# Local and pooled attention with a dense layer behind it: q and k of two more groups transposed by DMA, less slack behind transfers that VectorE reads, and new tables of who copies what

## The chip, the core and the metric

The kernel runs on one core of a Trainium2 chip. The metric is the device time of one execution in microseconds (us). The profile shows one such execution by engine: PE is TensorE, PEld its weight loads, DVE is VectorE, ACT is ScalarE, POOL is GpSimd and SP is SyncE, which here issues every transfer.

## The reference

q, k and v have the shape (8, 8, 576, 64): 8 batches, 8 heads, 576 positions, 64 wide. Each head's attention is the sum of two parts, and a dense layer follows.

```python
# pooled: mean over 4 neighbours, full attention over 144 positions, repeated 4 times
q_d = q.reshape(B, H, Sd, 4, D).mean(axis=3)          # k_d and v_d likewise
out_up = np.repeat(sm_attn(q_d, k_d, v_d), 4, axis=2)
# local: only positions with |i - j| < 4
scores = np.where(mask, scale * q @ k.T, -1e9)
out_local = softmax(scores) @ v
x = (out_up + out_local)      # as (4608 tokens, 512)
# dense
h = x @ w_in                  # 512 -> 2048
g = h - np.tanh(h)
return g @ w_out              # 2048 -> 512
```

## The kernel before

The 64 heads are worked on in 32 pairs (p), two pairs making a group (n), 16 groups in all. The instructions are not written in their final order. Each goes into a list with its engine, an assumed duration and what it reads and writes, and a list scheduler then lays down one fixed order for each engine. The scheduler's view of a transfer is its cost, a fixed 1800 ns, and a slack that keeps the reader from being placed too near:

```python
LAT = {"PE": 270, "ACT": 150, "DVE": 110, "POOL": 150, "SP": 50, "DMA": 1800}
...
lag = self.LAT[eng]
if self.ops[u][4] < 5000:                     # the reader's priority
    lag += self.spare(self.ops[u][4], eng, self.ops[u][0])
...
def spare(pri, eng, to):
    if eng == "DMA":
        return 2500 if pri >= 140 else 1500 if pri >= 80 else 0
    level = (pri >= 120) + (pri >= LATER)     # LATER = 180
    return SPARE[to == "PE"].get(eng, (0, 0, 0))[level]
```

An attention pair has priority 10 p, the turn of a group's q and k 20 n, their loads' readers 20 n - 12. The dense matmuls have priority 5000, so they fill what attention leaves.

**q and k.** They are loaded with rows of nine positions (qkn), cast and reordered to bf16 (`reorder`, line 494, into qr) and then transposed (`turn`). Up to group FI - 1 TensorE does it, nine transposes into a PSUM bank; from group FI on it is a DMA transpose into a v buffer (vst) that is not needed any more. A copy with a strided read brings either into qk, and two sums make the pooled q and k:

```python
def turn(n, i):                               # i = 0: q and k of one half, 1: the other
    ps, po, ts, ox = banks_of(2 * n + i)
    if (n, i) in TB:
        ps, ts = po, ox                       # through ps_ox in place of ps_ts
    if n >= FI:
        b16 = vst[4 + i] ...
        op("SP", 900, lambda: nc.sync.dma_start_transpose(out=b16..., in_=qr[s][:, i]...), ...)
        op("DMA", T_IN, None, ..., pri=pri)
    def tr():
        for a in range(A6):                   # nine; line 523
            T.transpose(b16[:, 128*a:128*a+128], qr[s][:, i, a, :], ident)
    ...                                       # copy, line 532: whole or in two halves (TS)
    ...                                       # add1 line 536, add2 line 541: sums of 4 (AS, AD)
```

For groups from FI on, v has four buffers in place of six (`slot_v`).

**One pair.** Scores of the local part (`s1`, line 590) go into ps_ts, those of the last tile and the pooled part (`s2`, lines 590 and 609) into the same bank or, from pair MERGE on, into ps_ox, in one block with the next pair's `s1`. ScalarE takes the exponential (lines 626, 652, 655), VectorE multiplies by the mask (630, 659). The output matmuls (`outs`, lines 672 and 678) write ps_ox; VectorE takes the reciprocal (689) and normalises into ln (691). The way back to xT is one of three:

```python
if p >= XOUT:                                 # XOUT = 12
    nc.sync.dma_start_transpose(out=lnT[sl], in_=ln[sl]...)     # then two adds, line 711
elif p in UP:                                 # matmuls that add both parts (726, 731), copy (737)
else:                                         # transposes (747 to 751), copy (754), add (756)
```

**Dense.** For each block of 512 tokens, `mm1` makes 16 times four 128x512 matmuls (line 781), followed by tanh (789) and the subtraction into gT (792), and `mm2` makes the second product (line 835), copied out by ScalarE (846). Four PSUM banks, `ps_hy`, serve both. While attention's first pairs run, ps_ts1 and ps_ox1 stand there; the dense part takes these over in two halves, a tile for each bank (`dense_banks`). Line 1069 is a filler matmul on a constant, placed where the scheduler sees TensorE idle ahead of the dense part.

Of the kernel before, what the change touches and what calls it, by code (L numbers as in the profile page):

```python
# [11 lines left out]
ALU = mybir.AluOpType  # L12
# [3 lines left out]
class Program:  # L16
# [20 lines left out]
    def op(self, eng, ns, fn, reads=(), writes=(), pri=0):  # L37
        i = len(self.ops)
        deps = set()
        for key in reads:  # L40
            if key in self.last_write:
                deps.add(self.last_write[key])
        for key in writes:
            if key in self.last_write:
                deps.add(self.last_write[key])
            deps.update(self.readers.get(key, ()))
        for key in reads:
            self.readers.setdefault(key, set()).add(i)
        for key in writes:
            self.last_write[key] = i  # L50
            self.readers[key] = set()
        deps.discard(i)
        self.ops.append((eng, ns, fn, deps, pri))
        self.touch.append(set(reads) | set(writes))
        return i
# [108 lines left out]
def kernel(  # L164
# [55 lines left out]
    vd = fixed("vd", [128, 2, 4, 65], BF16, NVW)  # L220
# [7 lines left out]
    lnT = fixed("lnT", [128, 7, 128], BF16, NLN)  # L228
    od = fixed("od", [128, G], BF16, 2)
# [25 lines left out]
    P = Program()  # L255

    def spare(pri, eng, to):
        if eng == "DMA":
            return 2500 if pri >= 140 else 1500 if pri >= 80 else 0
        level = (pri >= 120) + (pri >= LATER)  # L260
        return SPARE[to == "PE"].get(eng, (0, 0, 0))[level]
    LATER = 180
    SPARE = ({"POOL": (0, 500, 1000)},
             {"POOL": (0, 1000, 1500), "DVE": (0, 300, 800), "ACT": (0, 200, 500)})
    P.spare = spare
    op = P.op
    V, A, T, GP = nc.vector, nc.scalar, nc.tensor, nc.gpsimd
# [174 lines left out]
    def prep_v(p):  # L442
# [4 lines left out]
            out=vw[w][:, 2 * jj:2 * jj + 2, :, 0:64], in_=vst[s]))  # L447
                  for eng, ns, fn in CAST_V[CV.get(p, 1)]],
                 reads=[("vst", s, 0), ("vst", s, 1)],
# [49 lines left out]
    def turn(n, i):  # L499
# [4 lines left out]
        ps, po, ts, ox = banks_of(2 * n + i)  # L504
        if (n, i) in TB:
            ps, ts = po, ox
# [60 lines left out]
    def attention(p):  # L567
        b, j, hb, s, jj = p // NP, p % NP, p // 2, p % 2, p % 2
        w, sq, y, sl = hb % NVW, (p // 2) % 2, p % 2, p % NLN
        ps, po, ts, ox = banks_of(p)  # L570
        pri = 10 * p
# [47 lines left out]
        if p <= MERGE:  # L619
# [3 lines left out]
        e1 = E[se][:, 0:960].rearrange("p (h c) -> p h c", h=2)  # L623
# [4 lines left out]
           reads=ts, writes=[("E", se, 0)], pri=URG.get("e1", {}).get(p, pri))  # L628
        if not first:
# [3 lines left out]
                op=ALU.mult), reads=["mask"], writes=[("E", se, 0)], pri=pri)  # L633
# [11 lines left out]
        else:  # L645
            op("PE", 380 * cold, s2, reads=qks + qkds, writes=ox if p >= MERGE else ts,
               pri=pri)
        P.has(p // 2, ("qk", sq, 0), ("qk", sq, 1))
        if MERGE <= p < NPAIR - 1:
# [4 lines left out]
           reads=sb, writes=[("E", se, 1)], pri=URG.get("e2", {}).get(p, pri))  # L654
        op("ACT", 655, lambda: A.activation(
            out=e3, in_=pb[:, :, 96:384], func=AF.Exp, scale=SCALE / 16.0),
           reads=sb, writes=[("E", se, 2)], pri=URG.get("e2", {}).get(p, pri))
        if not first:
# [3 lines left out]
                op=ALU.mult), reads=["mask"], writes=[("E", se, 1)], pri=pri)  # L662
# [5 lines left out]
        def outs():  # L668
# [17 lines left out]
           reads=[("E", se, 0), ("E", se, 1), ("E", se, 2), ("vw", w, jj), ("vd", w)],  # L686
           writes=ox, pri=late)
        blocks = po[:, :, 0:455].rearrange("p h (n c) -> p h n c", c=65)
        op("DVE", 240, lambda: V.reciprocal(out=r[s], in_=blocks[:, :, :, 64]),
           reads=ox, writes=[("r", s)], pri=late)  # L690
# [4 lines left out]
            op=ALU.mult), reads=ox + [("r", s)], writes=[("ln", sl)],  # L695
           pri=URG.get("norm", {}).get(p, late))


        xo = xT[j][:, b * S:(b + 1) * S]
        if p >= XOUT:  # L700
            op("SP", 450, lambda: nc.sync.dma_start_transpose(
                out=lnT[sl], in_=ln[sl].rearrange("p n c -> p (n c)")),
               reads=[("ln", sl)], writes=[("lnT", sl), ("q", ("lnT", sl)), ("fl", p)],
               pri=pri - 60)
            op("DMA", T_OUT, None, reads=[("q", ("lnT", sl)), ("ln", sl)],
               writes=[("lnT", sl)], pri=pri)
            for t0, nt, n, up in ((0, 4, 120, lnT[sl][:, 5, 0:120]),
                                  (4, 1, 96, lnT[sl][:, 6, 104:128])):
                g = n // 4
                P.choice([(name, ns[t0 > 0], lambda eng=eng, t0=t0, nt=nt, n=n, g=g,  # L710
                           up=up: eng.tensor_tensor(  # L711
                    out=xo[:, QW * t0:QW * t0 + nt * n].rearrange(
                        "p (t g a) -> p t g a", t=nt, a=4),
                    in0=lnT[sl][:, t0:t0 + nt, 0:n].rearrange(
                        "p t (g a) -> p t g a", a=4),
                    in1=up[:, 0:nt * g].rearrange("p (t g) -> p t g", g=g).unsqueeze(3)
                    .to_broadcast([128, nt, g, 4]), op=ALU.add))
                          for name, ns, eng in XADD],
                         reads=[("lnT", sl)], writes=[("x", b, j)], pri=pri)
            return  # L720


        if p in UP:
# [11 lines left out]
            for m, (i0, i1) in enumerate([(0, 1), (1, 2)] if parted else [(0, 2)]):  # L735
# [4 lines left out]
                         reads=ox, writes=[(("x", "xh")[m], b, j)],  # L740
                         pri=URG.get("add", {}).get(p, late))
# [4 lines left out]
        def back():  # L746
# [8 lines left out]
           reads=ox, writes=[("od", s)], pri=URG.get("od", {}).get(p, late))  # L755
# [4 lines left out]
           reads=ox + [("od", s)], writes=[("x", b, j)],  # L760
           pri=URG.get("add", {}).get(p, late))
# [92 lines left out]
    def dense(kb):  # L854
# [18 lines left out]
        if kb == NBLK:  # L873
# [2 lines left out]

    M2_FIRST = 16
    XOUT, T_OUT, AHEAD = 12, 1600, 7
    P_A, LATE = 5000, {0: 40, 2: 40, 3: 40}
    MERGE, GV = 14, 7  # L880
    FI, T_IN = 11, 2050
    XADD = [("DVE", (800, 350), V)]
    ORDER, W_FIRST = '0g123', '0123qv'
    TB = {(1, 0), (1, 1), (2, 0), (2, 1), (3, 0), (5, 0)}
    PV = {2: 0, 3: 1, 4: -1, 5: 0, 6: 1}
    PLACE = {2: (0, 2), 3: (1, 2), 4: (4, 4), 5: (1, 2), 6: (4, 4), 7: (1, 1), 8: (3, 3)}
    W_LATE = [0, 0, 0, 0]
    T_QK, T_V, T_W, W_PRI = 900, 780, 2750, 53
    CAST = [("POOL", 620, GP.tensor_copy), ("ACT", 620, A.copy),
# [1 line left out]
    CAST_V = [[("POOL", 790, GP.tensor_copy), ("ACT", 720, A.copy)],  # L891
              [("POOL", 790, GP.tensor_copy)], [("ACT", 720, A.copy)],
              [("DVE", 500, V.tensor_copy)]]
    CV = {0: 3, 1: 1, 2: 1, 3: 3, 4: 1, 5: 0, 6: 3, 7: 0, 8: 2, 9: 0, 10: 2, 11: 3}
    REORDER = [[("DVE", 860, V.tensor_copy), ("ACT", 950, A.copy),
                ("POOL", 1350, GP.tensor_copy)],
               [("DVE", 860, V.tensor_copy)], [("ACT", 950, A.copy)],
               [("DVE", 1150, V.tensor_copy)], [("POOL", 1350, GP.tensor_copy)]]
    RE = {(0, 0): 1, (0, 1): 4, (1, 0): 2, (1, 1): 4, (2, 0): 3, (2, 1): 4, (3, 0): 0, (3,
          1): 0, (4, 0): 2, (4, 1): 4, (5, 0): 1, (5, 1): 1}  # L900
    TURN = [[("ACT", 1125, A.copy), ("DVE", 1250, V.tensor_copy)],
            [("ACT", 1125, A.copy)], [("DVE", 1250, V.tensor_copy)],
            [("ACT", 2210, A.copy)]]
    TU = {(0, 0): 2, (0, 1): 1, (1, 0): 2, (1, 1): 1, (2, 0): 1, (2, 1): 1, (3, 0): 2, (3,
          1): 1, (4, 0): 1, (4, 1): 1, (5, 0): 1, (5, 1): 1}
    re_v, re_a, re_p = (("DVE", 480, V.tensor_copy), ("ACT", 580, A.copy),
                        ("POOL", 720, GP.tensor_copy))
    REORDER_H = [[[re_v, re_a, re_p]] * 2, [[re_v], [re_a]], [[re_v], [re_p]],
# [1 line left out]
    POOLED = [[("ACT", 600, A.copy), ("DVE", 650, V.tensor_copy)],  # L910
              [("ACT", 600, A.copy)], [("DVE", 650, V.tensor_copy)]]
    PV1 = False
    VD = {0: 2, 1: 0, 2: 1, 3: 1, 4: 1, 5: 0, 6: 1}
    RS = {(0, 1): 2, (1, 0): 4, (1, 1): 3, (3, 0): 4}
    UP = {0: 3, 1: 0, 2: 3, 3: 3, 4: 2, 6: 3, 8: 1, 11: 3}
    UP_COPY = [("ACT", 660, A.copy), ("DVE", 720, V.tensor_copy)]
    UP_H = [[("ACT", 370, A.copy)], [("DVE", 410, V.tensor_copy)]]
    half_v, half_p = ("DVE", 420, 260, V), ("POOL", 650, 500, GP)
# [2 lines left out]
              [[("DVE", 700, V.tensor_copy)], [("ACT", 640, A.copy)]]]  # L921
    ADD_H = [[[half_v, half_p]] * 2, [[half_v], [half_p]], [[half_v], [half_v]],
             [[half_p], [half_p]]]
    TS = {(0, 0): 1, (0, 1): 2, (1, 1): 2, (2, 1): 2, (5, 0): 1, (5, 1): 3}
    AS = {(0, 0): 1, (1, 0): 1, (1, 1): 1, (2, 0): 1, (4, 0): 1, (5, 0): 4, (5, 1): 4, (6,
          1): 1}
    URG = {'e1': {8: -2, 9: -2, 10: -2, 11: -2}, 'e2': {0: -2, 1: -2, 2: -2, 3: -2, 4: -2,
          5: -2, 6: -2, 7: -2, 8: -2, 9: -2, 10: -2, 11: -2}, 'od': {0: -2, 1: -2}, 'norm':
          {0: -2, 1: -2, 2: -2, 3: -2, 4: -2, 5: -2, 6: -2, 7: -2, 8: -2, 9: -2, 10: -2, 11:
          -2}, 'add': {0: -2, 1: -2, 2: -2, 3: -2, 4: -2, 5: -2, 6: -2, 7: -2}, 'turn': {4:  # L930
          -2, 5: -2}, 'vd': {2: -2, 3: -2}}
    ADDERS = [[("DVE", 760, 440, V), ("POOL", 1190, 850, GP)],
              [("POOL", 1190, 880, GP)], [("DVE", 760, 440, V)]]
    AD = {(0, 0): 2, (0, 1): 2, (1, 0): 0, (1, 1): 1, (2, 0): 0, (2, 1): 1, (3, 0): 0, (3,
          1): 1, (4, 0): 0, (4, 1): 0, (5, 0): 2, (5, 1): 1}

    op("DVE", 180, lambda: V.memset(warm, 0.0), writes=["warm"], pri=-999)
    op("POOL", 500, c_ident, writes=["ident"], pri=-99)
# [5 lines left out]
    for i in range(2):  # L944
        def guards(i=i):
# [3 lines left out]
           writes=[("qk", i, a, y) for a in range(2) for y in range(2)])  # L949
    for i in range(NVW):  # L950
        def ones(i=i):
# [3 lines left out]
           writes=[("vd", i), ("vw", i, 0), ("vw", i, 1)])  # L955
# [3 lines left out]
           writes=[("vd", i)], pri=-96)  # L959
# [69 lines left out]
    for p in range(NPAIR):  # L1029
        n = p // 2  # L1030
        if p % 2 == 0 and 1 < n < GV and PV.get(n, 0) == 0:
            pool_v(n)
# [4 lines left out]
        def turns(at):  # L1037
            for m in range(max(n + 1, 2), min(n + 3, NGRP)):
                for i in range(2):
                    if 4 * m - 5 + PLACE.get(m, (0, 1))[i] == at:  # L1040
                        reorder(m, i)
                        turn(m, i)
        turns(2 * p)
        if p % 2 == 0 and 1 < n < GV and PV.get(n, 0) == 1:
            pool_v(n)
# [9 lines left out]
        if p % NP == NP - 1:  # L1055
            b = p // NP
# [44 lines left out]
```

## Time and profile before

| What | Value |
|---|---|
| time, median of 3 (lowest, highest) | 338.79 us (337.65, 339.12) |
| span of the profiled execution | 335.9 us |
| VectorE, subtraction into gT (L792) | 144, 684 ns each |
| ScalarE, tanh (L789) | 144, 601 ns each |
| q/k transposes on TensorE (L523) | 198 |
| q/k transposes by DMA (L514) | 10, landing 4.3 us after issue |
| transposes back by DMA (L701) | 20, landing 3.0 us after issue |
| transfers on SyncE's queue | 60.04 MB, 66.7% of 16 engines |

A row of the table of groups reads: line, engine, operation, what it writes and reads, how many | busy us, mean ns of one | idle time of the engine just before it, and what ended it. In a timeline a row is start, length, engine, line and operation; a bracket at its end is how long the engine stood idle before it, and behind what. Consecutive matmuls overlap in the records, so the pace of TensorE is read from starts.

### The profile page before, as it was taken

The numbers are of one execution on the slowest core, as the hardware profiler recorded it, in microseconds if no ns is written. First come the engines' busy times: TensorE is split into PE (matmuls) and PEld (weight loads), VectorE is DVE, ScalarE is ACT, GpSimd is POOL, SyncE is SP. The second block draws the span as 40 slices with busy tenths as digits, with TensorE's granted clock in tenths as the row PEclk, the third lists the DMA queues.
The fourth block names the chain that finished last, engine by engine and source line by source line (L and its number), as shares of the span: only waits on it lengthen the run. The fifth ranks groups of instructions, "written<-read, shape, count | busy, mean of one in ns | idle before, by whom it ended". The sixth has DMA issues, their size and how long they took to land.

```text
span 335.9 us, 6861 instructions
## 1 busy us (share of the span) xinstructions
PE 322.9 (96%) x2602; PEld 167.8 (50%) x2602; DVE 236.0 (70%) x388; ACT 211.2 (63%) x341; POOL 153.0 (46%) x181
## 2 busy tenths in 40 slices
PE   8778999989998999999999999999999999999996
PEld 5454554655554455554444544444444444444444
DVE  3788897679998888989797878787666444343300
ACT  1765878777848578667869695987554334344421
POOL 8564565349499488794948476653000000000000
PEclk9999999999999999999999999999999999999999
DMA  6999999999952799899899979843223100100012
GB/s 208 263 379 311 318 320 303 241 283 295 291 177 75 187 210 282 202 218 280 212 246 276 195 228 225 173 94 92 59 61 86 34 31 31 62 33 31 31 66 93
DMA packets 96878, 60.47 MB, mean 180 GB/s; under 512 B 74510, under 2 KB 80078, under 8 KB 96846
## 3 DMA queue, kind: packets, MB, share of 16 engines
q1 hardware_dynamic: 96846, 60.04, 66.7%
q8 instruction: 20, 0.33, 0.5%
q14 instruction: 12, 0.10, 0.1%
HBM read 43.05 MB, written 9.44 MB: 156 GB/s over the span
## 4 chain that ended last, share of the span: by engine, by line
PE 84%; DVE 10%; POOL 2%; issue 2%; ACT 1%; POOLq 0%; DVEq 0%
PE ps_hy L835 34%; PE ps_hy L781 33%; DVE ln L691 3%; PE ps_ox L672 3%; PE ps_ts L590 3%; PE ps_ts L523 2%; PE ps_ox L678 2%; PE ps_ts L1069 2%; DVE gT L792 2%; DVE qk L532 2%; PE ps_hy L810 1%; PE ps_ox L465 1%; DVE E L630 1%; POOL half L536 1%; ACT qk L532 1%
## 5 line engine op out<-in xcount | busy, mean ns | idle before, releaser
L781 PE MATMUL ps_hy<-xT,w_in_sb 128*128 128x512 bf16 x576 | 145.2, 379 | 0.6 <-DVE gT L792 0.4
L835 PE MATMUL ps_hy<-w_out_sb,gT 128*128 128x512 bf16 x560 | 140.4, 379 | 0.0
L792 DVE TENSOR_TENSOR gT<-ps_hy,uy 128x512 bf16<-128x512 f32 x144 | 94.9, 684 | 56.8 <-ACT uy L789 56.6
L789 ACT ACTIVATE uy<-ps_hy 128x512 f32<-128x512 f32 x144 | 83.0, 601 | 60.6 <-PE ps_hy L781 58.3
L781 PEld LDWEIGHTS <-w_in_sb 128*128 128x128 bf16 x576 | 53.1, 98 | 60.4 <-issue 1.8
L835 PEld LDWEIGHTS <-gT 128*128 128x128 bf16 x560 | 52.3, 98 | 57.6
L536 POOL TENSOR_TENSOR half<-qk 128x576 f32<-128x576 bf16 (+1 forms) x32 | 32.6, 1021 | 49.3 <-ACT qk L532 38.9
L691 DVE TENSOR_TENSOR ln<-ps_ox,r 128x896 bf16<-128x896 f32 x30 | 32.7, 1089 | 0.8
L626 ACT ACTIVATE E<-ps_ts 128x960 bf16<-128x960 f32 x30 | 29.4, 981 | 2.5 <-PE ps_ts L590 2.5
L846 ACT COPY uy<-ps_hy 128x512 f32<-128x512 f32 x35 | 20.6, 590 | 14.3 <-PE ps_hy L835 14.2
L630 DVE TENSOR_TENSOR E<-E,mask 128x960 bf16<-128x960 bf16 x28 | 24.5, 874 | 5.5 <-ACT E L626 5.4
L532 ACT COPY qk<-ps_ts 128x1152 bf16<-128x1152 bf16 (+1 forms) x16 | 16.5, 1034 | 18.0 <-PE ps_ts L523 8.3
L711 DVE TENSOR_TENSOR xT<-lnT 128x480 bf16<-128x480 bf16 (+1 forms) x40 | 27.6, 705 | 0.0
L359 POOL TENSOR_TENSOR qkn<-qkn 128x512 f32<-128x512 f32 (+1 forms) x18 | 25.8, 1432 | 3.3 <-DMA qkn<-in_v_dram 2.6
L446 POOL CAST vw<-vst 128x640 bf16<-128x640 f32 x26 | 22.9, 885 | 6.9 <-DMA vst<-in_v_dram 3.6
L494 POOL CAST qr<-qkn 128x1152 bf16<-128x1152 f32 (+1 forms) x16 | 19.4, 1214 | 8.4 <-DMA qkn<-in_k_dram 5.6
L532 ACT COPY qk<-vst 128x1152 bf16<-128x1152 bf16 x10 | 22.1, 2209 | 0.9 <-POOL half L536 0.9
L541 POOL TENSOR_TENSOR qkd<-half 128x288 bf16<-128x288 f32 (+1 forms) x32 | 21.4, 673 | 1.6 <-DVE half L536 0.4
L672 PE MATMUL ps_ox<-vw,E 128*128 128x65 bf16 x300 | 18.2, 194 | 1.9 <-DVE qk L532 1.0
L672 PEld LDWEIGHTS <-E 128*128 128x128 bf16 x300 | 15.4, 98 | 9.0 <-issue 2.3
L590 PEld LDWEIGHTS <-qk 64*128 64x128 bf16 x320 | 9.6, 95 | 18.2 <-issue 15.2
L494 DVE CAST qr<-qkn 128x1152 bf16<-128x1152 f32 (+1 forms) x16 | 15.4, 965 | 2.2 <-DMA qkn<-in_q_dram 2.2
(106 smaller groups left out, 294.5 us busy)
## 6 DMA issues: line engine op xcount, KB each, us to landing
vst<-in_v_dram SPq DMA_DIRECT2D x62, 160.0 KB, 4.9
qkn<-in_q_dram SPq DMA_DIRECT2D x32, 288.0 KB, 4.1
qkn<-in_k_dram SPq DMA_DIRECT2D x32, 288.0 KB, 4.9
out_dram<-uy SPq DMA_DIRECT2D x35, 256.0 KB, 3.5
qkn<-in_v_dram SPq DMA_DIRECT2D x9, 512.0 KB, 5.1
gT<-in_moe_w_in_dram SPq DMA_DIRECT2D x4, 1024.0 KB, 9.1
xT<-in_moe_w_out_dram SPq DMA_DIRECT2D x8, 256.0 KB, 4.6
gT<-in_moe_w_out_dram SPq DMA_DIRECT2D x2, 1024.0 KB, 8.9
```

The costliest lines, as they stand in the source:

```text
L494: P.choice([(eng, ns, lambda fn=fn, x0=x0, x1=x1: fn(out=dst[:, x0:x1], in_=srt[:, x0:x1])) for eng, ns, fn in table], reads=[("qkn", sn, ...
L532: fn(out=o[:, ys].rearrange("p y (g a) -> p y g a", a=A6), in_=b16.rearrange("p (a g y) -> p y g a", a=A6, y=2)[:, ys])
L536: eng.tensor_tensor(out=half[:, ys], in0=four[:, ys, :, 0:2], in1=four[:, ys, :, 2:4], op=ALU.add)
L626: op("ACT", 980, lambda: A.activation(out=e1, in_=ps[:, :, 0:480], func=AF.Exp, scale=SCALE), reads=ts, writes=[("E", se, 0)], pri=URG.get ...
L630: op("DVE", 900, lambda: V.tensor_tensor(out=e1, in0=e1, in1=mask[:, 0:480].unsqueeze(1).to_broadcast([128, 2, 480]), op=ALU.mult), reads= ...
L672: T.matmul(po[:, hh, 65 * t:65 * t + 65], E[se][:, c:c + 128], vw[w][:, 2 * jj + hh, t, :], start=True, stop=True)
L691: op("DVE", 1090, lambda: V.tensor_tensor(out=ln[sl].rearrange("p n (h d) -> p h n d", d=D), in0=blocks[:, :, :, 0:64], in1=r[s].unsqueeze ...
L711: up=up: eng.tensor_tensor(out=xo[:, QW * t0:QW * t0 + nt * n].rearrange("p (t g a) -> p t g a", t=nt, a=4), in0=lnT[sl][:, t0:t0 + nt, 0: ...
L781: T.matmul(ps_hy[slot], w_in_sb[:, dc, fc * 128:(fc + 1) * 128], xT[dc][:, kb * 512:kb * 512 + 512], start=(dc == 0), stop=(dc == N_DC - 1))
L789: op("ACT", 490, lambda: A.activation(out=u[us], in_=ps_hy[slot], func=AF.Tanh), reads=[("hy", slot)], writes=[("u", us)], pri=-1)
L792: op("DVE", 620, lambda: V.tensor_tensor(out=gT[g][:, fc, :], in0=ps_hy[slot], in1=u[us], op=ALU.subtract), reads=[("hy", slot), ("u", us) ...
L835: T.matmul(ps_hy[slot], gT[g][:, fc, ts * 128:ts * 128 + 128], w_out_sb[:, fc, :], start=(fc == 0), stop=(fc == N_FF - 1))
```

## The change

Two more groups, 9 and 10, have q and k transposed by DMA (FI from 11 to 9). A transfer that VectorE reads gets a slack of 1000 ns where it had 1500 or 2500; readers on other engines keep theirs. Scores are merged from pair 13 in place of 14 (MERGE). The turn of group 5 leaves ps_ox (TB). The pairs whose outputs are held back at the start are 1 and 2 with priority 25, where they were 0, 2 and 3 with 40 (LATE). The remaining tables say which engine copies or adds which group's data, whole or in halves, where in the program a turn is written down, and what is urgent; they are drawn anew so that the order fits the new slack. The purpose is to take transposes off TensorE and to let the DMA transposes back be used sooner.

```diff
     def spare(pri, eng, to):
+        if eng == "DMA" and to == "DVE":
+            return NEAR if pri >= 80 else 0
         if eng == "DMA":
             return 2500 if pri >= 140 else 1500 if pri >= 80 else 0
...
-    LATER = 180
+    LATER = 200
+    NEAR = 1000
...
-    P_A, LATE = 5000, {0: 40, 2: 40, 3: 40}
-    MERGE, GV = 14, 7
-    FI, T_IN = 11, 2050
-    XADD = [("DVE", (800, 350), V)]
+    P_A, LATE = 5000, {1: 25, 2: 25}
+    MERGE, GV = 13, 7
+    FI, T_IN = 9, 2050
...
-    TB = {(1, 0), (1, 1), (2, 0), (2, 1), (3, 0), (5, 0)}
-    PV = {2: 0, 3: 1, 4: -1, 5: 0, 6: 1}
-    PLACE = {2: (0, 2), 3: (1, 2), 4: (4, 4), 5: (1, 2), 6: (4, 4), 7: (1, 1), 8: (3, 3)}
+    TB = {(1, 0), (1, 1), (2, 0), (2, 1), (3, 0)}
+    PV = {2: 0, 3: 0, 4: -1, 5: -1, 6: 0}
+    PLACE = {2: (0, 0), 3: (1, 2), 4: (4, 4), 5: (1, 2), 6: (4, 4), 7: (1, 1), 8: (2, 2)}
...                      # CV, RE, TU, VD: who casts v, reorders, copies a turn, pooled v
-    UP = {0: 3, 1: 0, 2: 3, 3: 3, 4: 2, 6: 3, 8: 1, 11: 3}
+    UP = {0: 2, 1: 0, 2: 1, 3: 3, 4: 2, 6: 3, 8: 0, 11: 3}
...
-    TS = {(0, 0): 1, (0, 1): 2, (1, 1): 2, (2, 1): 2, (5, 0): 1, (5, 1): 3}
+    TS = {(0, 0): 3, (0, 1): 1, (1, 1): 1, (2, 1): 1, (4, 0): 1, (4, 1): 3, (5, 0): 3, (5,
+          1): 2, (6, 1): 1}
...                      # RS, AS, AD: halves of the reorder, who adds; URG: what is urgent
```

The choice in XADD had one entry, VectorE, and becomes a plain instruction on VectorE. In UP, 3 is a copy in two halves on ScalarE and VectorE, 1 a whole copy on ScalarE, 2 a whole one on VectorE, 0 leaves it to the scheduler.

More of the change, by code (lines that the diff above doesn't have):

```diff
@@ L709, in attention @@
                 g = n // 4
-                P.choice([(name, ns[t0 > 0], lambda eng=eng, t0=t0, nt=nt, n=n, g=g,
-                           up=up: eng.tensor_tensor(
+                op("DVE", (800, 350)[t0 > 0], lambda t0=t0, nt=nt, n=n, g=g, up=up: V.tensor_tensor(
                     out=xo[:, QW * t0:QW * t0 + nt * n].rearrange(
@@ L716, in attention @@
                     in1=up[:, 0:nt * g].rearrange("p (t g) -> p t g", g=g).unsqueeze(3)
-                    .to_broadcast([128, nt, g, 4]), op=ALU.add))
-                          for name, ns, eng in XADD],
-                         reads=[("lnT", sl)], writes=[("x", b, j)], pri=pri)
+                    .to_broadcast([128, nt, g, 4]), op=ALU.add),
+                   reads=[("lnT", sl)], writes=[("x", b, j)], pri=pri)
             return
@@ L893 @@
               [("DVE", 500, V.tensor_copy)]]
-    CV = {0: 3, 1: 1, 2: 1, 3: 3, 4: 1, 5: 0, 6: 3, 7: 0, 8: 2, 9: 0, 10: 2, 11: 3}
+    CV = {0: 3, 1: 1, 2: 2, 3: 3, 4: 0, 5: 1, 6: 3, 7: 1, 8: 2, 9: 0, 10: 0, 11: 3}
     REORDER = [[("DVE", 860, V.tensor_copy), ("ACT", 950, A.copy),
@@ L898 @@
                [("DVE", 1150, V.tensor_copy)], [("POOL", 1350, GP.tensor_copy)]]
-    RE = {(0, 0): 1, (0, 1): 4, (1, 0): 2, (1, 1): 4, (2, 0): 3, (2, 1): 4, (3, 0): 0, (3,
-          1): 0, (4, 0): 2, (4, 1): 4, (5, 0): 1, (5, 1): 1}
+    RE = {(0, 0): 0, (0, 1): 1, (1, 0): 4, (1, 1): 2, (2, 0): 1, (2, 1): 0, (3, 0): 4, (3,
+          1): 0, (4, 0): 2, (4, 1): 4, (5, 0): 0, (5, 1): 1}
     TURN = [[("ACT", 1125, A.copy), ("DVE", 1250, V.tensor_copy)],
@@ L903 @@
             [("ACT", 2210, A.copy)]]
-    TU = {(0, 0): 2, (0, 1): 1, (1, 0): 2, (1, 1): 1, (2, 0): 1, (2, 1): 1, (3, 0): 2, (3,
-          1): 1, (4, 0): 1, (4, 1): 1, (5, 0): 1, (5, 1): 1}
+    TU = {(0, 0): 0, (0, 1): 1, (1, 0): 0, (1, 1): 2, (2, 0): 0, (2, 1): 2, (3, 0): 0, (3,
+          1): 0, (4, 0): 0, (4, 1): 2, (5, 0): 2, (5, 1): 0}
     re_v, re_a, re_p = (("DVE", 480, V.tensor_copy), ("ACT", 580, A.copy),
@@ L912 @@
     PV1 = False
-    VD = {0: 2, 1: 0, 2: 1, 3: 1, 4: 1, 5: 0, 6: 1}
-    RS = {(0, 1): 2, (1, 0): 4, (1, 1): 3, (3, 0): 4}
-    UP = {0: 3, 1: 0, 2: 3, 3: 3, 4: 2, 6: 3, 8: 1, 11: 3}
+    VD = {0: 2, 1: 1, 2: 1, 3: 0, 4: 0, 5: 2, 6: 1}
+    RS = {(0, 1): 2, (1, 1): 3, (2, 1): 1, (3, 0): 4}
+    UP = {0: 2, 1: 0, 2: 1, 3: 3, 4: 2, 6: 3, 8: 0, 11: 3}
     UP_COPY = [("ACT", 660, A.copy), ("DVE", 720, V.tensor_copy)]
@@ L923 @@
              [[half_p], [half_p]]]
-    TS = {(0, 0): 1, (0, 1): 2, (1, 1): 2, (2, 1): 2, (5, 0): 1, (5, 1): 3}
[L925 to L931, printed above, removed]
+    TS = {(0, 0): 3, (0, 1): 1, (1, 1): 1, (2, 1): 1, (4, 0): 1, (4, 1): 3, (5, 0): 3, (5,
+          1): 2, (6, 1): 1}
+    AS = {(0, 0): 1, (1, 0): 1, (1, 1): 1, (2, 0): 1, (2, 1): 2, (3, 0): 4, (5, 0): 4, (5,
+          1): 4, (6, 1): 2}
+    URG = {'e1': {0: -2, 1: -2}, 'e2': {0: -2, 1: -2, 2: -2, 3: -2, 4: -2, 5: -2, 6: -2, 7:
+          -2, 8: -2, 9: -2, 10: -2, 11: -2}, 'od': {0: -2, 1: -2, 2: -2, 3: -2, 4: -2, 5:
+          -2, 6: -2, 7: -2}, 'norm': {8: -2, 9: -2, 10: -2, 11: -2}, 'add': {0: -2, 1: -2},
+          'turn': {4: -2, 5: -2}, 'vd': {4: -2, 5: -2}}
     ADDERS = [[("DVE", 760, 440, V), ("POOL", 1190, 850, GP)],
               [("POOL", 1190, 880, GP)], [("DVE", 760, 440, V)]]
-    AD = {(0, 0): 2, (0, 1): 2, (1, 0): 0, (1, 1): 1, (2, 0): 0, (2, 1): 1, (3, 0): 0, (3,
-          1): 1, (4, 0): 0, (4, 1): 0, (5, 0): 2, (5, 1): 1}
+    AD = {(0, 0): 0, (0, 1): 2, (1, 0): 0, (1, 1): 1, (2, 0): 0, (2, 1): 0, (3, 0): 2, (3,
+          1): 1, (4, 0): 1, (4, 1): 0, (5, 0): 2, (5, 1): 0}
     op("DVE", 180, lambda: V.memset(warm, 0.0), writes=["warm"], pri=-999)
```

## The prediction

> **What bounds the kernel now.** I read the page first, for who is busy and when.
>
> ```profile
> PE 322.9 (96%) x2602; PEld 167.8 (50%) x2602; DVE 236.0 (70%) x388; ACT 211.2 (63%) x341; POOL 153.0 (46%) x181
> ...
> PE   8778999989998999999999999999999999999996
> ...
> PE 84%; DVE 10%; POOL 2%; issue 2%; ACT 1%; POOLq 0%; DVEq 0%
> ```
>
> TensorE is busy 322.9 of 335.9 us and carries 84% of the chain that ended last. The dense part is the bulk: in the table of groups the two 128x512 matmuls stand with 576 and 560, and in the timeline four of them in a row take 0.86 us, so 0.2157 us each and 1136 x 0.2157 = 245 us. A time on this kernel can therefore come from two places only: TensorE work that goes away, and the 13.0 us in which TensorE is idle. Where is that idle time? The stretches of 12 us say it; the columns are the length, then busy us of PE, PEld, DVE, ACT and POOL.
>
> ```profile
> 0.00:12.00 12.00, 9.36 (x64) 5.84 (x64) 4.95 (x24) 3.16 (x5) 10.77 (x28) 1.00 0.81 235
> 12.00:24.00 12.00, 9.54 (x148) 6.51 (x149) 10.86 (x18) 9.10 (x17) 5.51 (x9) 1.00 1.06 320
> 24.00:36.00 12.00, 10.49 (x98) 5.74 (x95) 10.29 (x19) 7.43 (x15) 5.50 (x9) 1.00 1.04 319
> ...
> 72.00:84.00 12.00, 10.66 (x119) 5.71 (x118) 11.11 (x17) 9.90 (x19) 9.55 (x14) 1.00 1.05 290
> ...
> 96.00:108.00 12.00, 10.61 (x117) 6.17 (x115) 10.75 (x16) 7.44 (x13) 11.76 (x13) 1.00 0.45 131
> 108.00:120.00 12.00, 12.00 (x111) 6.25 (x110) 10.65 (x17) 7.58 (x13) 7.17 (x7) 1.00 0.80 216
> ```
>
> The head (0 to 36 us) holds 2.64 + 2.46 + 1.51 = 6.6 us of idle, the last stretch 2.9 us, and everything between 3.5 us, of which 1.34 lie at 72 to 84 us and 1.39 at 96 to 108 us. From 108 us to the last output tile TensorE waits for 0.17 us in all. So after 108 us the kernel is a queue of TensorE work: what is taken out of it is gained in full, as long as nothing comes late to it.
>
> **What the Trainium skill says.** *TensorE: Matmul & The Clock Gate*, section "Wait — 56ns, not 53.3ns?", gives starts of warm matmuls 55.6 ns apart at 128 columns and 215.7 ns at 512. The trace agrees: 0.2157 us for the dense ones, and 0.50 us for nine transposes. The page's 219 ns for one of them (table of groups) is pipelined; *Perfetto Trace Analysis*, section "Tensor Engine Instruction (MATMUL, LD_WEIGHTS)", says that the end of a TensorE instruction is estimated, so I take distances between starts. *VectorE: DVE Perf Modes*, section "The three transpose paths", lists 390 ns for a 128x128 transpose on TensorE, into PSUM, and 1309 ns by DMA, into SBUF. Here a DMA transpose of nine such blocks lands after 4.3 us, which is less than nine times that, but on a queue where TensorE does not wait if it was issued in time. *SBUF — State Buffer*, section "SBUF: two separate sides", says that VectorE and GpSimd share a pair of ports that one holds for a whole instruction; the trace fits, as the add that makes xT from lnT takes 186 to 1569 ns.
>
> **Part 1, q and k of groups 9 and 10 by DMA.** FI falls from 11 to 9: two groups, two tensors each, so 4 x 9 = 36 TensorE transposes go. The order of instructions has 198 of them before and 162 after. What does one turn of nine cost?
>
> ```profile
> 129.08 0.67 PE L523 MATMUL ps_ts<-ident,qr 128*128 128x128 bf16 x9
> 129.58 0.59 PE L835 MATMUL ps_hy<-w_out_sb,gT 128*128 128x512 bf16 x2
> ```
>
> The next matmul starts 0.50 us later; the other three turns of these groups (at 124.55, 138.22 and 144.38) give 0.51, 0.51 and 0.50. Sum: **2.0 us off TensorE**, all in the stretch where it is never idle. What it adds lies beside: four DMA transposes, and four copies on ScalarE whose source is now SBUF.
>
> ```profile
> L532 ACT COPY qk<-vst 128x1152 bf16<-128x1152 bf16 x10 | 22.1, 2209 | 0.9 <-POOL half L536 0.9
> L532 ACT COPY qk<-ps_ts 128x1152 bf16<-128x1152 bf16 x13 | 14.6, 1125 | 9.2 <-PE ps_ts L523 6.3 <-POOL half L536 2.9
> ```
>
> Four at 2.21 for four at 1.125 us is 4.3 us more on ScalarE, in a stretch (120 to 150 us) where it is busy 5.8 to 8.5 of every 10 us. The groups from 11 on already run this way with no TensorE wait, so I count no cost.
>
> **Part 2, no transposes into the bank ps_ox in group 5.** TB loses (5,0). Two waits hang on it:
>
> ```profile
> 73.02 0.39 PE L590 MATMUL ps_ts<-qk 64*128 64x120 bf16 x8 [0.23 <-ACT qk L532]
> ...
> 75.33 0.32 PE L672 MATMUL ps_ox<-vw,E 128*128 128x65 bf16 x5 [0.95 <-DVE qk L532]
> ```
>
> The output matmuls write ps_ox, and wait until both half copies have emptied the turn that stood there. After the change both turns of group 5 go through ps_ts, 12 dense matmuls apart, and the output matmuls wait for neither; but the second turn is followed, after only 4 dense matmuls and one set of outputs (4 x 0.216 + 0.5 = 1.36 us), by scores that need it. Its two half copies took 0.64 on ScalarE and 0.76 on VectorE, one after the other, so about 1.4 us plus hand-overs: I leave 0.5 us of new wait. **1.18 - 0.5 = 0.7 us gained.**
>
> **Part 3, the transposes back of pair 10.** At 97.70 TensorE waits for the add that empties ps_ox:
>
> ```profile
> 97.70 0.32 PE L672 MATMUL ps_ox<-vw,E 128*128 128x65 bf16 x5 [0.51 <-DVE xT L756]
> ```
>
> Before, 10 dense matmuls stood between those transposes and these outputs; after, 16 do (1.3 us more), and on VectorE the add stands ahead of the other work. **0.5 us gained.** The two waits of 0.44 us at 102 us stand in the same order in both kernels and stay.
>
> **Part 4, merged scores from pair 13.** One pair more has its scores in one block. Each change to 64-row matmuls leaves 0.10 us (two dense matmuls start at 109.17, end by their pace at 109.60, the scores start at 109.70). **0.1 us.**
>
> **Part 5, the head.** VectorE is the busy engine from 12.9 to 20.6 us. One of its 0.30 us sums moves to GpSimd, and the whole copy of the first xT on it (0.75) replaces a wait of 0.54 and a half copy of 0.46. I count **0.2 us**; the chain of four normalisations (1.09 + 0.24 each) that ends the head is the same.
>
> **Part 6, the slack and the tables.** With NEAR = 1000 the list scheduler puts VectorE work on a landed transfer 1.5 us (priority 140 on) or 0.5 us sooner. No time comes of it where TensorE is full; it tightens. The last xT shows how much there is: outputs end at 255.9, its DMA transpose is issued at 258.04, lands some 3.0 us later, near 261, and the add starts at 264.26. That leaves 3 us, of which 1.5 may go. The other tables (who copies, who adds) move whole instructions between engines; ScalarE gains 4 us, VectorE and GpSimd less than 1 us. I expect some new short waits in 36 to 108 us, where the old tables left 3.5 us of them, and set **0.7 us** against the gains.
>
> **Sum.** -2.0 - 0.7 - 0.5 - 0.1 - 0.2 + 0.7 = -2.8 us, from 338.8: **336.0 us**.
>
> **Rivals.** *A: nothing is gained, because each reordering opens as many waits as it closes.* For it: the stretch 72 to 108 us has VectorE at about 11 of every 12 us, and every table there was re-drawn. Against: the 2.0 us of Part 1 lie after 108 us, where 0.17 us of waits stand. It would leave 337 to 338 us. *B: the transfers become the bound.* The DMA share is 0.77 to 1.10 in each 10 us from 110 to 220 us, and four more transposes, with an issue of about 2 us each on the one queue, go in ahead of the loads; loads late by some us would stop attention, and TensorE with it, since its order is fixed. Against: it is as full from 150 to 210 us, with the same transposes in, and no wait. It would make 340 us or more. *C: VectorE waits for a transfer placed too near* and holds back the subtractions that free the dense banks. For it: its queue is in order. Against: the 3 us found above. It would cost 1 to 2 us. *D: more comes than counted*, if the waits at 72 to 108 us close altogether: 334 us.
>
> **Range and chances.** The certain term is 2.0 us, known to 0.1; the rest is +-2 us, and the three times before spread over 1.5 us. So 333.8 to 338.8 us. Faster by 2% would be below 332.0, more than all waits between head and end; slower by 2% is above 345.6 and needs rival B at large.
>
> **What the profile after would show.** Part 1: 162 transposes in place of 198, no TensorE wait over 0.2 us after 108 us, PE busy time down by more than 2 us. Parts 2 and 3: no wait of the outputs for a qk copy near 75 us or for the add near 97 us; in their place at most 0.5 us of scores waiting for qk. Part 5: the first dense matmul of the long run near 28.8 instead of 28.96 us. Rival B would show as TensorE idle behind E, vw or qk between 110 and 230 us; rival C as VectorE idle ahead of the xT add until a DMA. I am wrong if the loads slip, or if the new tables in 36 to 108 us leave more than 5 us of idle.

## The result, and the profile after

The changed kernel takes 334.44 us (median of 4, 333.76 to 335.05) where the kernel before takes 338.8 in the same rounds: a ratio of 0.9877 (95% interval 0.9846 to 0.9907), 4.2 us. A second measurement beside other kernels gave 0.9878 (0.9847 to 0.9910). The predicted 336.0 us was 1.6 us too high; the measured time lies inside the stated range.

First the page of the kernel after. Lines past the first change of the source bear other numbers: L523 is now L526, L532 L535, L590 L593, L672 L675, L781 L782, L792 L793.

```profile
PE 320.9 (97%) x2564; PEld 166.2 (50%) x2564; DVE 231.0 (69%) x387; ACT 214.0 (64%) x341; POOL 154.3 (46%) x185
...
PE   8778999999999999999999999999999999999996
...
PE 88%; DVE 7%; ACT 2%; issue 2%; POOL 1%; DVEq 0%; POOLq 0%; ACTq 0%
```

TensorE has 2.0 us less to do, its row of tenths has lost the two 8s between head and end, and more of the last chain is TensorE's own. The span fell from 335.9 to 332.5 us, so 1.4 us of idle went as well. The stretches of 12 us show where (length, then busy us of PE, PEld, DVE, ACT, POOL, then the clock, the DMA share and GB/s):

```profile
0.00:12.00 12.00, 9.68 (x63) 6.08 (x64) 4.89 (x25) 2.49 (x3) 10.77 (x27) 1.00 0.80 232
12.00:24.00 12.00, 9.45 (x147) 6.36 (x145) 10.60 (x18) 9.35 (x16) 5.35 (x9) 1.00 1.03 315
24.00:36.00 12.00, 10.62 (x101) 5.84 (x98) 10.46 (x19) 8.30 (x16) 5.30 (x8) 1.00 1.02 320
...
60.00:72.00 12.00, 11.18 (x124) 6.84 (x123) 9.63 (x15) 7.24 (x14) 8.25 (x9) 1.00 0.94 256
72.00:84.00 12.00, 11.83 (x132) 6.66 (x131) 10.83 (x18) 10.16 (x20) 8.45 (x12) 1.00 1.05 277
...
96.00:108.00 12.00, 11.29 (x115) 6.48 (x112) 10.79 (x17) 7.43 (x12) 11.25 (x13) 1.00 0.72 199
108.00:120.00 12.00, 12.00 (x124) 6.63 (x123) 8.88 (x16) 8.65 (x15) 6.45 (x8) 1.00 1.00 235
120.00:132.00 12.00, 12.00 (x111) 6.07 (x110) 11.91 (x18) 11.04 (x15) 10.93 (x11) 1.00 1.10 257
```

Between 36 and 108 us TensorE is idle for 2.3 us where it was for 3.3; from 108 us on it is nothing again (0.04 us at 204 to 216 us). Look at 120 to 132 us: VectorE 11.9, ScalarE 11.0 and GpSimd 10.9 of 12 us busy, and TensorE does not wait. Three of the six waits that still stop TensorE there, from its timeline (start, length, then the idle time before it and its releaser in brackets); the others are 0.22, 0.33 and 0.20 us:

```profile
66.65 0.39 PE L593 MATMUL ps_ts<-qk 64*128 64x120 bf16 x8 [0.68 <-ACT qk L535]
...
75.48 0.39 PE L593 MATMUL ps_ts<-qk 64*128 64x120 bf16 x8 [0.17 <-ACT qk L535]
...
101.84 0.72 PE L468 MATMUL ps_ox<-vw,pick 128*128 128x256 bf16 x5 [0.44 <-DVE xT L738]
```

The 0.95 us of outputs waiting for a copy and the 0.51 us of outputs waiting for an add are gone. The scores of group 5 wait 0.17 us; those of group 4 now wait 0.68 us at 66.65, because they too stand four dense matmuls and one set of outputs behind a turn of nine in the same bank. The copies, from the table of groups (busy, mean ns | idle before, releaser):

```profile
L535 ACT COPY qk<-vst 128x1152 bf16<-128x1152 bf16 x14 | 31.3, 2234 | 0.4 <-POOL half L539 0.4
...
L535 ACT COPY qk<-ps_ts 128x576 bf16<-128x576 bf16 (+1 forms) x14 | 11.8, 847 | 17.4 <-DVE qk L535 12.2
```

Four more of them come from the v buffer, at 2.23 us each.

**The head, like for like.** The first transposes of q and k start between 6.54 and 8.02 us in the profiles of this study. Ahead of them every kernel has the same 29 filler matmuls; these start 0.267 us apart at first and 0.136 us apart from some moment on. The slow ones number 11 in the profile before, 17 in that after and up to 22 in others, 0.13 us lost with each, so up to 1.5 us go by here whatever the change. The profile before had an early start (6.56 us), that after a later one (7.31), so "28.91 against 28.96 us" for the long run of dense matmuls hides a gain. From the first matmul that pools v to that long run it is 11.04 or 11.05 us in all six profiles with the old order of the head, and 10.53 to 10.57 us in six of the eight with the new one (10.91 and 11.21 in the other two): 0.5 us.

### The profile page after: what moved, and what is told of

The parts are those of the page before. It is cut to its first block, busy times and chain, and to the rows that moved or that the text cites. A ratio compares the mean times of both kernels' runs of the same rounds, so it can differ in the third digit from the quotient of the medians.

```text
span 332.5 us, 6791 instructions
## 1 busy us (share of the span) xinstructions
PE 320.9 (97%) x2564; PEld 166.2 (50%) x2564; DVE 231.0 (69%) x387; ACT 214.0 (64%) x341; POOL 154.3 (46%) x185
## 4 chain that ended last, share of the span: by engine, by line
PE 88%; DVE 7%; ACT 2%; issue 2%; POOL 1%; DVEq 0%; POOLq 0%; ACTq 0%
PE ps_hy L782 36%; PE ps_hy L836 35%; PE ps_ts L593 3%; PE ps_ox L675 2%; PE ps_ts L1069 2%; PE ps_ox L681 2%; DVE qk L535 2%; PE ps_ts L526 2%; DVE ln L694 1%; ACT qk L535 1%; PE ps_hy L811 1%; POOL half L539 1%; PE ps_ox L468 1%; PE ps_ox L612 1%; PE ps_ox L526 1%
## 5 line engine op out<-in xcount | busy, mean ns | idle before, releaser
L782 PE MATMUL ps_hy<-xT,w_in_sb 128*128 128x512 bf16 x576 | 145.7, 379 | 0.2
L793 DVE TENSOR_TENSOR gT<-ps_hy,uy 128x512 bf16<-128x512 f32 x144 | 95.5, 684 | 55.4 <-ACT uy L790 54.5
L782 PEld LDWEIGHTS <-w_in_sb 128*128 128x128 bf16 x576 | 53.3, 98 | 59.8 <-issue 0.6
L539 POOL TENSOR_TENSOR half<-qk 128x576 f32<-128x576 bf16 (+1 forms) x33 | 33.9, 1029 | 43.7 <-ACT qk L535 33.3
L535 ACT COPY qk<-vst 128x1152 bf16<-128x1152 bf16 x14 | 31.3, 2234 | 0.4 <-POOL half L539 0.4
L544 POOL TENSOR_TENSOR qkd<-half 128x288 bf16<-128x288 f32 (+1 forms) x35 | 23.5, 676 | 4.8 <-DVE half L539 3.4
L713 DVE TENSOR_TENSOR xT<-lnT 128x480 bf16<-128x480 bf16 (+1 forms) x40 | 23.6, 617 | 1.1 <-DMA lnT<-ln 1.1
L449 POOL CAST vw<-vst 128x640 bf16<-128x640 f32 x25 | 19.5, 782 | 8.4 <-DMA vst<-in_v_dram 8.2
L535 ACT COPY qk<-ps_ts 128x576 bf16<-128x576 bf16 (+1 forms) x14 | 11.8, 847 | 17.4 <-DVE qk L535 12.2
L497 POOL CAST qr<-qkn 128x1152 bf16<-128x1152 f32 (+1 forms) x16 | 18.5, 1159 | 5.8 <-DMA qkn<-in_k_dram 1.9
L593 PEld LDWEIGHTS <-qk 64*128 64x128 bf16 x320 | 9.8, 95 | 18.4 <-issue 13.5
L675 PEld LDWEIGHTS <-E 128*128 128x128 bf16 x300 | 15.3, 98 | 7.0 <-issue 0.8
L675 PE MATMUL ps_ox<-vw,E 128*128 128x65 bf16 x300 | 18.1, 194 | 0.6 <-DVE vd L475 0.6
L681 PE MATMUL ps_ox<-vd,E 128*128 128x65 bf16 x240 | 16.9, 192 | 0.0
```

What stands on the lines that cost most here:

```text
L535: fn(out=o[:, ys].rearrange("p y (g a) -> p y g a", a=A6), in_=b16.rearrange("p (a g y) -> p y g a", a=A6, y=2)[:, ys])
L539: eng.tensor_tensor(out=half[:, ys], in0=four[:, ys, :, 0:2], in1=four[:, ys, :, 2:4], op=ALU.add)
L675: T.matmul(po[:, hh, 65 * t:65 * t + 65], E[se][:, c:c + 128], vw[w][:, 2 * jj + hh, t, :], start=True, stop=True)
L713: op("DVE", (800, 350)[t0 > 0], lambda t0=t0, nt=nt, n=n, g=g, up=up: V.tensor_tensor(out=xo[:, QW * t0:QW * t0 + nt * n].rearrange("p (t ...
L782: T.matmul(ps_hy[slot], w_in_sb[:, dc, fc * 128:(fc + 1) * 128], xT[dc][:, kb * 512:kb * 512 + 512], start=(dc == 0), stop=(dc == N_DC - 1))
L793: op("DVE", 620, lambda: V.tensor_tensor(out=gT[g][:, fc, :], in0=ps_hy[slot], in1=u[us], op=ALU.subtract), reads=[("hy", slot), ("u", us) ...
```

## The experiments

Three theories stood against each other. The **queue** theory: past 108 us TensorE is a full queue, and its work counts in full. The **transfers** theory: the loads slip behind the transposes. And, from the misses of the first runs on, the **VectorE queue** theory: VectorE carries out its list in order, and where the list puts several long instructions ahead of a subtraction into gT, TensorE waits for the dense bank. Ratios are to the kernel before, in the same rounds; us are the ratio's distance from 1 times 338. In the traces of several of these runs some dense matmuls have no record (2525 to 2596 where 2566 to 2638 weight loads stand), which shows as idle of 0.16 us "until issue"; those are not counted as waits.

**1. The transposes of groups 9 and 10 twice, the order untouched** (the kernel before with)

```diff
-            for a in range(A6):
+            for a in list(range(A6)) * (2 if n in (9, 10) else 1):
```

> The kernel before, with the nine TensorE transposes of each turn of groups 9 and 10 issued twice (the second time over the first, same result); every engine keeps its order. Theory (from about 108 us on TensorE is a full queue, so its work counts in full): 36 more transposes at 0.056 us make it 2.0 us slower, 340.8 where before is 338.8, and the turns' starts to the next matmul grow from 0.50 to 1.0 us. Rival (these transposes hide beside waits of other engines, the gain came from the new tables alone): under 0.5 us slower.

Measured: 1.0047 (1.0032 to 1.0062), 1.6 us slower (1.1 to 2.1). The turn's timeline:

```profile
124.00 1.18 PE L523 MATMUL ps_ts<-ident,qr 128*128 128x128 bf16 x18
125.01 1.46 PE L835 MATMUL ps_hy<-w_out_sb,gT 128*128 128x512 bf16 x6
```

The turn takes 1.01 us in place of 0.50, and the interval holds the expected 2.0 us. Behind the turns one wait of before (0.17 us for E near 141 us) is gone. The waits of 0.16 and 0.28 us near 83 and 87 us are absent too, though every engine's order is that of before and the doubled turns come later: these two come and go with the execution. The transposes are not hidden; the queue theory holds.

**2. FI = 9 alone** (old tables, old slack)

```diff
-    FI, T_IN = 11, 2050
+    FI, T_IN = 9, 2050
```

> The kernel before with FI = 9 alone: groups 9 and 10 by DMA, old tables, old slack. Theory: 2.0 us faster (336.8 where before is 338.8), no wait of TensorE over 0.3 us after 108 us. Rival, transfers bound: loads slip behind the four transposes, TensorE waits for vw, qk or E between 120 and 220 us, same time or slower. Rival, tables alone: no change.

Measured: 1.0034 (1.0018 to 1.0050), 1.1 us *slower*. Neither expectation fits: the transposes are gone, and no wait names a load. Four waits of TensorE past 108 us came up, 1.80, 0.19, 0.77 and 0.44 us, 3.2 us in all; less the 2.0 us and the 0.17 us of waits before, this is 1.0 of the 1.1 us. Two of them, 1.80 and 0.77 us, name the subtraction. Here is the longest: first TensorE's line, then VectorE's list ahead of it, then GpSimd's.

```profile
158.71 0.59 PE L781 MATMUL ps_hy<-xT,w_in_sb 128*128 128x512 bf16 x2 [1.80 <-DVE gT L792]
```

```profile
155.49 0.24 DVE L711 TENSOR_TENSOR xT<-lnT 128x96 bf16<-128x96 bf16 x1
155.66 1.29 DVE L494 CAST qr<-qkn 128x1152 bf16<-128x1152 f32 x1
156.87 1.19 DVE L659 TENSOR_TENSOR E<-E,mask 128x192 bf16<-128x192 bf16 x1
157.98 0.68 DVE L792 TENSOR_TENSOR gT<-ps_hy,uy 128x512 bf16<-128x512 f32 x1
```

```profile
156.39 1.55 POOL L494 CAST qr<-qkn 128x1152 bf16<-128x1152 f32 x1
```

The subtraction's tanh was done at 156.68 us. It stands behind a multiplication by the mask, which takes 0.48 us on average in the kernel before (0.24 to 0.26 where GpSimd runs nothing beside it) and here takes 1.19: it ends at 158.06, 0.112 us (by the unrounded times) after GpSimd's cast, which ends at 157.94. FI also decides from which group on v has four buffers; no run separates that from the transposes, but neither TensorE nor VectorE waits for a transfer here past 108 us.

**3. Group 5's turn out of ps_ox alone** (the kernel before, TB without (5, 0))

```diff
-    TB = {(1, 0), (1, 1), (2, 0), (2, 1), (3, 0), (5, 0)}
+    TB = {(1, 0), (1, 1), (2, 0), (2, 1), (3, 0)}
```

> The kernel before with group 5's turn moved out of ps_ox (TB without (5,0)) alone. Theory: the waits of 0.23 and 0.95 us near 73 and 75 us go and up to 0.5 us of scores waiting for qk comes: 0.7 us faster. Rival (waits are only moved, because the two turns now stand one behind the other in ps_ts): within 0.3 us of before.

Measured: 0.9953 (0.9926 to 0.9980), 1.6 us faster (0.7 to 2.5), which does not exclude the expected 0.7. The waits of 0.23 and 0.95 us are gone, and so are those of 0.51 us near 97 and 0.44 us near 102 us, which I had not counted on. New are these two:

```profile
93.38 0.39 PE L590 MATMUL ps_ts<-qk 64*128 64x120 bf16 x8 [0.58 <-ACT qk L532]
...
142.22 1.02 PE L781 MATMUL ps_hy<-xT,w_in_sb 128*128 128x512 bf16 x4 [0.88 <-DVE gT L792]
```

One entry of a table moves whole stretches of the order, for the better and for the worse.

**4. The slack alone** (the kernel before)

```diff
+        if eng == "DMA" and to == "DVE":
+            return NEAR if pri >= 80 else 0
...
-    LATER = 180
+    LATER = 200
+    NEAR = 1000
```

> The kernel before with the slack alone (1000 ns behind transfers that VectorE reads, LATER 200), old tables, FI 11. Theory: TensorE is full where these transfers are read, so within 0.3 us of before; the adds of xT start about 1.5 us sooner behind their transposes. Rival (the slack is what brings the time): 1 us or more faster. Rival C (VectorE stands waiting for a transfer): slower by 1 to 2 us, with VectorE idle ahead of the xT add until a DMA.

Measured: 0.9984 (0.9968 to 0.9999), 0.5 us faster. No VectorE wait for a transfer past the head, none of TensorE past 108 us. On the old tables the slack is worth little, as expected. LATER, changed with it, is not a slack behind transfers: a reader whose priority lies below it gets a smaller slack behind results of GpSimd, and on TensorE also behind those of VectorE and ScalarE. With 200, pairs 18 and 19 and the turn of group 9 (priorities 180 and 190) get the smaller one too.

**5. The changed kernel with FI back at 11**

> The changed kernel with FI back at 11 (groups 9 and 10 transposed on TensorE again), all else as changed. Theory (2.0 us of TensorE work, counting in full, if the order brings no new wait): 2.0 us slower than the changed kernel, that is 2.4 us faster than before (0.993). Rival (the DMA transposes are worth nothing by themselves, as with FI alone on the old tables, where waits of TensorE for VectorE's subtraction took the gain back): within 0.7 us of the changed kernel, 0.986 to 0.989.

```diff
-    FI, T_IN = 9, 2050
+    FI, T_IN = 11, 2050
```

Measured: 0.9967 (0.9954 to 0.9980), 3.0 us slower than the changed kernel (0.9878; 1.9 to 4.1 by the two intervals). 2.0 us of it are the transposes; waits for the subtraction of 0.77 us near 86 and 0.33 us near 167 us can account for the rest. On the new tables the two groups by DMA are worth at least about what was predicted.

**6. The changed kernel with the old slack** (both lines of the slack taken out, LATER = 180)

> The changed kernel with the old slack (1500 or 2500 ns behind every transfer, LATER 180), all tables and FI 9 as changed. Theory: the slack alone is worth 0 to 0.5 us, so 0 to 0.5 us slower than the changed kernel (0.987 to 0.989 of before). Rival (the little slack is what keeps VectorE's queue from jamming where FI is 9): waits of TensorE for the subtraction of 1 us or more between 140 and 220 us, 1.5 us or more slower than the changed kernel (0.992 and up).

Measured: 0.9984 (0.9970 to 0.9998), 3.6 us slower than the changed kernel. The rival of the expectation came true; three waits past 108 us, 2.7 us together:

```profile
156.47 0.59 PE L780 MATMUL ps_hy<-xT,w_in_sb 128*128 128x512 bf16 x2 [1.11 <-DVE gT L791]
...
205.22 0.59 PE L780 MATMUL ps_hy<-xT,w_in_sb 128*128 128x512 bf16 x2 [0.67 <-ACT uy L845]
209.00 0.59 PE L780 MATMUL ps_hy<-xT,w_in_sb 128*128 128x512 bf16 x2 [0.90 <-DVE gT L791]
```

The first is the picture of experiment 2: a mask multiplication of 1.19 us ahead of the subtraction, ending 0.112 us after a cast on GpSimd.

```profile
154.15 1.55 POOL L495 CAST qr<-qkn 128x1152 bf16<-128x1152 f32 x1
...
154.63 1.19 DVE L660 TENSOR_TENSOR E<-E,mask 128x192 bf16<-128x192 bf16 x1
```

This run sets back two things, the slack behind transfers and LATER; experiment 10 takes them apart.

**7 and 8. One and two groups more by DMA** (the changed kernel with FI = 8 and FI = 7)

> The changed kernel with FI 8: one group more by DMA. Theory: 18 more transposes go from TensorE, 1.0 us faster than the changed kernel (0.984 of before) if no wait comes. Rival, transfers bound: the DMA share is already 1.0 to 1.2 from 108 to 204 us; loads slip, TensorE waits behind vw or qk, 1 us or more slower than the changed kernel. Rival, VectorE's queue: waits for the subtraction, as with FI alone on the old tables.

> The changed kernel with FI 7: two groups more by DMA. Theory: 2.0 us faster than the changed kernel (0.981 of before) if no wait comes. Rival, transfers bound: a DMA share at its ceiling from 96 us on and TensorE waiting behind loads; slower than the changed kernel by 2 us or more, and by more than with FI 8.

Measured: 0.9934 (0.9912 to 0.9956) with 8, 0.9988 (0.9972 to 1.0004) with 7; 1.9 and 3.7 us slower than the changed kernel. The waits of TensorE past 108 us are 2.2 us with FI 8 and 2.8 us with FI 7, where 1.7 us more lie at 101 and 106 us. All of them name the subtraction, ScalarE's copy out of a dense bank, a qk copy or a mask multiplication; none names a load. VectorE waits for a DMA transpose back once, 0.4 us, with FI 8, and not at all with FI 7. The mean DMA share from 144 to 216 us with FI 7 is 1.14, that of the stretches of the changed kernel up to 1.20. The times answer as if transfers were the bound, but the waits do not name them. The waits do not explain all of it: in the profiles the spans are 1.8 and 3.3 us longer than that of the changed kernel. More waits less the transposes saved come to 0.6 and 1.5 us, and the long run of dense matmuls starts 0.7 and 1.1 us later. The rest, some 0.5 to 0.7 us, stays open.

**9. Two instructions of VectorE exchanged** (the kernel of experiment 2; in the finished order, the subtraction of 158 us goes ahead of the mask multiplication)

```diff
         order = self.order()
+        # 58th subtraction into gT: the mask multiplication just ahead of it goes behind it
+        self.swap(order, 57)
...                                     # swap exchanges two entries of VectorE's list
```

> The kernel before with FI = 9 alone, and one pair of VectorE's instructions exchanged: the subtraction that ended TensorE's wait of 1.80 us near 159 us now stands ahead of the mask multiplication that ran 1.19 us beside GpSimd's cast. Theory (VectorE's queue jams there, its two-input SBUF work held until GpSimd's cast ends): the subtraction runs right behind the cast of q, and the wait falls to 0.8 us or less; about 1 us faster than FI = 9 alone, that is 1.000 of before. Rival (TensorE waits there for a late transfer or for ScalarE): the wait stays above 1.5 us, 1.003 of before.

VectorE in that stretch:

```profile
153.88 1.28 DVE L504 CAST qr<-qkn 128x1152 bf16<-128x1152 f32 x1
155.09 0.67 DVE L802 TENSOR_TENSOR gT<-ps_hy,uy 128x512 bf16<-128x512 f32 x1
155.69 0.59 DVE L669 TENSOR_TENSOR E<-E,mask 128x192 bf16<-128x192 bf16 x1
```

GpSimd beside it, then TensorE:

```profile
154.62 1.55 POOL L504 CAST qr<-qkn 128x1152 bf16<-128x1152 f32 x1
```

```profile
155.82 0.59 PE L791 MATMUL ps_hy<-xT,w_in_sb 128*128 128x512 bf16 x2 [0.68 <-DVE gT L802]
```

The wait falls from 1.80 to 0.68 us, as the VectorE queue theory said. The whole kernel: 1.0023 (1.0003 to 1.0043) where experiment 2 has 1.0034; 0.4 us better, with intervals that overlap, so the expected 1 us is not shown by the times. The other three waits (0.19, 0.76, 0.44 us) stand as before.

**10. The short slack behind loads only**

> The changed kernel with the slack of 1000 ns for loads that VectorE reads only; behind the DMA transposes back it is 1500 or 2500 ns again. Theory (the little slack counts behind the transposes back, as the other half of it, on loads, leaves every engine's order as in the changed kernel): TensorE waits for the subtraction come back, 1 us or more between 140 and 220 us, 0.993 of before or more. Rival (LATER = 200, which stays here, is what counted): within 0.7 us of the changed kernel, under 0.990.

```diff
-        if eng == "DMA" and to == "DVE":
+        if eng == "DMA" and to == "DVE" and pri % 10 != 0:
```

Measured: 0.9909 (0.9882 to 0.9936), 1.0 us slower than the changed kernel, with intervals that overlap; one wait past 108 us, 0.61 us for the subtraction near 207 us. Between both expectations: with the long slack behind the transposes back one wait returns, but not the 2.7 us of experiment 6. The loads' part of the slack changes nothing: with the long slack behind every transfer and LATER = 200 the scheduler lays down the same five orders as in this experiment, and with the short slack behind the transposes back only, those of the changed kernel. So experiment 6 (0.9984) and this one (0.9909) differ by LATER alone, and LATER is worth 2.5 us of the 3.6; the short slack behind the transposes back is worth the other 1.0, which the intervals do not make certain.

**11. FI 8 with ScalarE's copies in halves**

> The changed kernel with FI 8, and ScalarE's copies of q and k from the v buffer in two halves of about 1.1 us in place of one of 2.2, so that a tanh or a copy out can go between. Theory (the waits with FI 8 come from work held behind long instructions of ScalarE and VectorE): waits of TensorE for ScalarE's copy out (0.63 and 0.19 us with FI 8) go, 0.5 to 1 us faster than FI 8 and so near the changed kernel, 0.988 to 0.991; it beats the changed kernel only if the waits for the subtraction go too. Rival, transfers bound: no better than FI 8, 0.993.

```diff
-        parted = TS.get((n, i), 0)
+        parted = 9 if n >= FI else TS.get((n, i), 0)
...
-            table = (TURN_H[parted - 1][k] if parted else
+            table = ([("ACT", 1130, A.copy)] if parted == 9 else
+                     TURN_H[parted - 1][k] if parted else
```

Measured: 1.0009 (0.9994 to 1.0024), 2.5 us slower than FI 8. Of the two waits for ScalarE's copy out one went (0.63 us near 133) and the other grew (0.19 to 0.72 us near 206), and the total past 108 us rose from 2.2 to 3.6 us. Neither expectation fits: it is not faster, and no wait of TensorE names a transfer.

**12. The changed kernel again**

> The changed kernel once more, in the same rounds as the three runs beside it, for a narrower interval. Expected: 0.985 to 0.990 of before; TensorE idle under 0.1 us between 108 us and the last stretch, and 10.5 us from the first matmul that pools v to the long run of dense matmuls, where before has 11.0.

Measured: 0.9878 (0.9847 to 0.9910), 333.37 us. No wait of TensorE past 108 us, 10.54 us in the stretch of the head. None of the variants beats it.

## Why the prediction was right, and where its steps were not

**Part 1, 2.0 us: right in size, wrong in "I count no cost".** Nine transposes cost TensorE 0.50 us (experiment 1: 0.51 more for nine more), they are not hidden, and taking them out is worth 3.0 us on the new tables. But alone, on the old tables, the same step *costs* 1.1 us (experiment 2). That "the groups from 11 on already run this way with no TensorE wait" did not carry over to groups 9 and 10: 3.2 us of waits came, 2.6 us of them for VectorE's subtraction behind a crowded list.

**Part 6, "No time comes of it": wrong.** On the old tables the slack is worth 0.5 us; with the old slack and the old LATER the changed kernel loses 3.6 us (experiment 6), through waits at the places where FI 9 alone brought them (156, 205 and 209 us; there 159, 207 and 211). Most of it, 2.5 us, is LATER, which the prediction did not name. So FI, slack and tables are not a sum of parts; the 2.0 us came where the order kept VectorE's subtractions clear, and were lost in experiments 2 and 6, where it did not.

**Parts 2 and 3 with the charge of Part 6, 0.5 us: too small.** The waits of both parts went as foreseen, 1.69 us. For new ones I set 0.5 + 0.7 us; 1.4 us came in the first profile after and 0.8 us in the second. But one of the two waits at 102 us that were to stay, 0.44 us of scores for a qk copy, went as well. Waits from 36 to 108 us sum to 3.3 us before (2.9 us in experiment 1, in the same order), 2.0 us in the first profile after and 1.5 us in the second: a gain of 0.9 to 1.8 us. Part 3 rested on 16 dense matmuls between the transposes back and the next outputs; that wait also vanishes with TB alone.

**Part 5, 0.2 us: mis-sized,** 0.5 us by the like-for-like stretch; the sign that it named, the start of the long run, could not show it, since the pace of the fillers moves that start by more. **Part 4, 0.1 us,** was not tested by itself.

The sum by what was measured, with Part 4's 0.1 as it was assumed: 2.0 + 0.9 to 1.8 + 0.5 + 0.1 = 3.5 to 4.4 us; the ratio says 4.2 (3.2 to 5.2). That the total came near is in part luck: Part 1's cost and Part 6 were wrong in opposite directions, since the order that the slack and the tables gave kept off the waits that FI brings by itself.

**The rivals.** A is refuted by experiments 1 and 5 for the transposes, though experiment 2 shows it at work when FI is changed alone. B did not happen: no TensorE wait named a load, even with FI 7. C showed once, VectorE waiting 1.1 us for a transpose back in the first profile after (not in the second), with nothing lost on TensorE. D happened in large part: the waits from 72 to 108 us fell from 3.0 us to 1.1 and 0.6 us, but 0.7 us came at 66 us.

## What to carry to other kernels

Where one engine is a full queue, price a removal by distances between starts, and then ask which *other* engine's in-order list must make room for what replaces it: here the transfers cost TensorE no wait, and VectorE's list did. In a list-scheduled kernel a constant of the model (a slack, a threshold) and the tables drawn with it are one setting: FI and the slack, each set or undone by itself, gave 0.5 to 3.6 us away from what was expected of it. When a profile is compared with another, compare stretches between the same two instructions, not clock times from the start.

## What the runs showed that I had not expected

- A VectorE multiplication of two SBUF operands, 128x192, takes 0.24 to 0.26 us in the 112 cases of the fourteen profiles in which GpSimd runs nothing beside it. In the 37 cases in which it starts while GpSimd still has over 0.2 us of a 128x1152 cast from float32 to go, it ends 0.105 to 0.114 us after the cast, and so takes 0.33 to 1.22 us. The Trainium skill, *SBUF — State Buffer*, section "SBUF: two separate sides", describes this: an exclusive hold of a shared pair of ports for a whole instruction. The subtraction, with one operand in PSUM, takes at most 0.694 us in all its 2016 records, also beside that cast (0.67 us in experiment 9). The scheduler counts 450 ns for the multiplication wherever it stands, so its order cannot foresee the hold. (The 186 to 1569 ns of the add in the prediction mix two shapes, 128x480 and 128x96.)
- The DMA transposes back land 4.5 us (median, 2.9 to 6.1) after issue in the changed kernel, where they took 3.0 us before; the 14 of q and k land after 5.2 us where 10 took 4.3. No wait of TensorE names one.
- The pace of the first 29 filler matmuls doubles anywhere from 4.05 to 6.99 us after the start of the span, with the same instructions ahead. That is 1.5 us in a comparison of 4.
